# A decode kernel bound by its K/V stream: MLP weights moved ahead of the stream, wo and w4 behind it, and PE's tile work written as a loop

## The chip, the cores and the metric

The kernel runs on one core of one Trainium2 chip. The metric is device time in microseconds (us). A kernel was run several times, and the kernel before was always run beside it on the same chip. Repeated runs of one kernel agree within 0.5% (most within 0.3%). Engines are named as the profile names them: PE (matrix products), PEld (its weight loads), DVE (vector), ACT (scalar), POOL and SP (here the engine that issues the transfers). "DMA engine" means one of the 16 hardware engines that carry the transfers of this core.

## The reference, cut to what matters

One token is decoded. There are two branches on the same normalised input, and both are added to it.

```python
xn = _layernorm(x)
# A: grouped-query attention over a cache: 32 query heads, 4 K/V heads, 65536 positions, width 128
q = xn @ wq                                   # 1024 x 4096
o = softmax(q k^T / sqrt(128)) v              # K and V: 67 MB each
A = o @ wo                                    # 4096 x 1024
# B: mixer MLP with one position, so the shifted h is all zeros
hs = shift(gelu(layernorm(xn) @ w1)) @ w2     # 1024 x 1024 each
x1 = xn + hs
B = x1 + gelu(layernorm(x1) @ w3) @ w4        # 1024 x 3584 and 3584 x 1024
return x + A + B
```

All data is bf16. 169.87 MB must be read and only 2 KB written.

## The kernel before

The cache is cut into 32 tiles (`NT`) of 8192 positions, and two tiles make one K transfer and one V transfer of 4 MB. DVE transposes each half of K into `X` (`Ttr`), PE forms the scores (`QK`), DVE and ACT do the running softmax, PE and DVE transpose the probabilities (`PTr`), PE multiplies them by V (`PV`), and POOL accumulates (`FLASH`). Each buffer `Kn` and `Vn` has two slots. The MLP and output weights travel between the K/V transfers into a buffer `W` of their own, and their products stand between the tiles:

```python
w_seq = [(0, w1_dma, 3, w1_pe), (4, w2_dma, 7, w2_pe),
         (8, lambda: w3_dma(0), 11, lambda: w3_pe(0)), (12, lambda: w3_dma(1), 15, lambda: w3_pe(1)),
         (16, lambda: wo_dma(0), 19, lambda: wo_pe(0)), (20, lambda: wo_dma(1), 23, lambda: wo_pe(1))]
...
for n in range(NT):
    h, nb = divmod(n, NSUB)
    QK(n); Ttr(n + 1, [0]); stats1(n)
    if nb == 0 and h > 0: combine_1(h - 1)          # the finished head, while the next one runs
    MB(n); stats2(n); EXP(n); Ttr(n + 1, [1])
    if nb == 0 and h > 0: combine_2(h - 1)
    PTr(n); Ttr(n + 1, [2, 3]); PV(n); FLASH(n)
    ...                                             # products and transfers of w_seq, next K or V
wo_pe(2); combine_1(3); combine_2(3); wo_pe(3)
for i in range(4): w4_pe(i)
```

The last pair of tiles is loaded in two halves each of K and V (`if m < NPAIR - 1: ... else: for hf in range(2)`).

## Time and profile before

| what | kernel before |
|---|---|
| time, median of 3 runs | 402.89 us (402.85 to 402.98) |
| profiled span | 401.7 us |
| data read | 169.87 MB |
| DMA engines busy, 13 to 385 us | 100% |
| last w4 part fully landed | 398.8 us |
| last product on PE ends | 399.4 us |

The page of the profile for the kernel before, parts 1 to 4 in extract. Part 1 gives the busy us of each engine (share of the span), part 2 the mean busy share of the DMA engines in 40 slices (9 is 90% or more), part 3 packets, MB and share of the 16 DMA engines' time by queue, part 4 the chain that ended last.

```profile
span 401.7 us, 4776 instructions
PE 186.4 (46%) x1859; PEld 78.5 (20%) x1875; DVE 228.4 (57%) x401; ACT 48.9 (12%) x128; POOL 61.8 (15%) x90
DMA  8999999999999999999999999999999999999994
...
q1 hardware_dynamic: 6920, 169.87, 98.4%
q8 instruction: 15, 0.25, 0.2%
q14 instruction: 8, 0.07, 0.0%
...
DMA 55%; DVE 24%; PE 16%; issue 2%; ACT 1%; SPq 0%; another core or an unknown queue 0%; POOL 0%; ACTq 0%
```

No compute engine is above 57%, and the DMA row has no hole between its first and last slice: the transfers set the time. The two ends can change it. The view by windows shows the far end. The columns are the window, its length, the busy us of PE, PEld, DVE, ACT and POOL with instruction counts, the granted share of PE's clock, the DMA share and GB/s.

```profile
390.00:393.00 3.00, 2.63 (x52) 1.74 (x56) 0.00 (x0) 0.00 (x0) 0.00 (x0) 0.50 0.97 412
393.00:396.00 3.00, 1.15 (x44) 0.69 (x36) 0.00 (x0) 0.00 (x0) 0.00 (x0) 0.99 0.88 371
396.00:399.00 3.00, 1.43 (x32) 0.48 (x24) 0.00 (x0) 0.00 (x0) 0.00 (x0) 0.58 0.32 128
399.00:402.00 3.00, 0.44 (x8) 0.00 (x0) 0.42 (x1) 0.00 (x0) 0.00 (x0) 0.50 0.00 1
```

The DMA share does not drop from 1 to 0 at once; it falls to 0.88 and 0.32 over 5 us. Some of the 16 DMA engines have finished their part while others have not, and a transfer is of use only when all have: the last product below starts at 398.85 us, 0.04 us after the last landing. The trace records 16 landings for each transfer, one for each DMA engine. These are the landings of one transfer near the start, one in the middle and the last w4 part, in us after the first of the 16:

```
lands at 32.2   0  0.05 0.11 0.12 0.16 0.17 0.20 0.23 0.25 0.26 0.27 0.29 0.30 0.32 0.33 0.38
lands at 234.6  0  0.11 0.24 0.29 0.33 0.66 0.85 1.53 1.57 1.61 1.61 1.63 1.64 1.67 1.68 1.87
lands at 398.8  0  0.10 0.15 0.21 0.43 0.71 1.12 1.31 1.58 2.79 2.86 2.89 2.90 2.94 2.98 3.44
```

The spread grows in steps, and each large step follows an instruction packet: the packet on queue q8 (16 KB of PE's program) holds one DMA engine for about 0.9 us, and the next 32 KB packet of that engine then takes, in most cases, about 1.7 us instead of 1.21.

The timeline of the tail (start, length, engine, line, operation, tiles, shapes, count, and in brackets the idle time before it and what ended it) shows the products of the last combine (which merges the partial sums of one K/V head), then PE waiting for each part of w4, then a copy; the store follows:

```profile
384.67 1.16 PE L564 MATMUL M_ps<-O_acc,cb_W 128*128 128x128 f32 x8 [0.78 <-DVE cb_W L557]
386.92 1.88 PE L404 MATMUL OUT_ps<-W,o_bf 128*1 128x256 bf16 x32 [1.09 <-DVE o_bf L571]
390.37 2.98 PE L404 MATMUL OUT_ps<-Kn,gh_bf 128*1 128x256 bf16 x56 [1.58 <-DMA Kn<-in_B_w_dram]
395.21 1.04 PE L404 MATMUL OUT_ps<-Kn,gh_bf 128*1 128x256 bf16 x32 [1.85 <-DMA Kn<-in_B_w_dram]
397.63 1.02 PE L404 MATMUL OUT_ps<-Kn,gh_bf 128*1 128x256 bf16 x16 [1.38 <-DMA Kn<-in_B_w_dram]
398.85 0.59 PE L404 MATMUL OUT_ps<-Kn,gh_bf 128*1 128x256 bf16 x8 [0.19 <-DMA Kn<-in_B_w_dram]
399.50 0.42 DVE L631 CAST orow<-OUT_ps 128x256 bf16<-128x256 f32 x1 [12.73 <-PE OUT_ps L404]
```

### The profile page before, as it was taken

To read this page: it belongs to the slowest core of one execution; us is meant where nothing else is said; L and a number is where in the kernel's file an instruction comes from. 1 tells how busy PE (TensorE), PEld (TensorE's weight loads), DVE (VectorE), ACT (ScalarE), POOL (GpSimd) and SP (SyncE) were. 2 spreads that over 40 slices of the span, in tenths; PEclk is the share of its full clock that TensorE was granted. 3 is DMA by queue.
4 is the path that set the end of the run, shared out by engine and by line. 5 is a ranking of instruction groups with operands and counts; after the bars stand their busy time and mean duration, and the time that the engine had idled before them with its cause. 6 is when DMAs were issued, how large, how long until landed. Compare 5 with 4: busy or idle time off the path is not lost.

```text
span 401.7 us, 4776 instructions
## 1 busy us (share of the span) xinstructions
PE 186.4 (46%) x1859; PEld 78.5 (20%) x1875; DVE 228.4 (57%) x401; ACT 48.9 (12%) x128; POOL 61.8 (15%) x90
## 2 busy tenths in 40 slices
PE   0332325064525745285531965353433654444664
PEld 0211101021103511062110731121111311111132
DVE  0247566277816578255744287576836775788410
ACT  1000111011101011011110011111201111112100
POOL 5000003012211011110310101111110112112110
PEclk9985556556565556555655555656555656565566
DMA  8999999999999999999999999999999999999994
GB/s 359 424 418 438 445 418 424 460 419 421 436 447 419 429 435 435 422 436 445 420 428 450 426 419 441 441 419 428 434 439 421 447 432 424 426 425 436 437 416 207
DMA packets 7087, 170.19 MB, mean 424 GB/s; under 512 B 916, under 2 KB 920, under 8 KB 1048
## 3 DMA queue, kind: packets, MB, share of 16 engines
q1 hardware_dynamic: 6920, 169.87, 98.4%
q8 instruction: 15, 0.25, 0.2%
q14 instruction: 8, 0.07, 0.0%
q10 hardware_dynamic: 144, 0.00, 0.0%
HBM read 169.87 MB, written 0.00 MB: 423 GB/s over the span
## 4 chain that ended last, share of the span: by engine, by line
DMA 55%; DVE 24%; PE 16%; issue 2%; ACT 1%; SPq 0%; another core or an unknown queue 0%; POOL 0%; ACTq 0%
DMA Kn<-in_A_k_cache_dram 44%; DVE X L476 13%; DMA Kn<-in_B_w_dram 6%; DMA Vn<-in_A_wq_dram 5%; PE H_ps L366 4%; PE S_ps L488 3%; DVE pT_f L529 3%; PE OT_ps L536 3%; DVE mrow L495 3%; PE M_ps L366 1%; ACT p_sb L518 1%; PE PT_ps L527 1%; PE M_ps L564 1%; PE OUT_ps L404 1%; DVE Yall L393 1%
## 5 line engine op out<-in xcount | busy, mean ns | idle before, releaser
L476 DVE STREAM_TRANSPOSE X<-Kn 128x1024 f32<-128x1024 f32 x128 | 151.7, 1215 | 67.4 <-DMA Kn<-in_A_k_cache_dram 67.4
L536 PE MATMUL OT_ps<-Vn,pT_f 128*32 128x512 bf16 x512 | 60.7, 627 | 52.4 <-DVE pT_f L529 52.4
L488 PE MATMUL S_ps<-X,Yall 128*32 128x512 bf16 x512 | 59.1, 608 | 16.1 <-DVE X L476 16.1
L501 PE MATMUL MB_ps<-Rm,Lmat 128*128 128x16 bf16 x32 | 6.1, 192 | 90.1 <-DVE Rm L496 90.1
L550 POOL TENSOR_TENSOR O_acc<-O_acc,tmpO 128x513 f32<-128x513 f32 x28 | 32.8, 1172 | 88.6 <-ACT tmpO L544 88.6
L518 ACT ACTIVATE p_sb<-S_ps,brun 128x512 bf16<-128x512 f32 x32 | 22.0, 687 | 192.7 <-DVE brun L516 157.3
L548 POOL TENSOR_SCALAR O_acc<-O_acc,ff 128x513 f32<-128x513 f32 x28 | 19.5, 698 | 153.4 <-ACT ff L523 153.4
L495 DVE TENSOR_REDUCE mrow<-S_ps 128x1 f32<-128x512 f32 x32 | 21.6, 674 | 25.5 <-PE S_ps L488 25.5
L544 ACT ACTIVATE tmpO<-OT_ps 128x512 f32<-128x512 f32 x32 | 19.1, 598 | 108.0 <-PE OT_ps L536 108.0
L488 PEld LDWEIGHTS S_ps<-X,Yall 128*32 128x32 bf16 x512 | 16.6, 126 | 54.7 <-DVE X L476 38.2
L529 DVE STREAM_TRANSPOSE pT_f<-PT_ps 128x512 f32<-128x512 f32 x32 | 22.9, 716 | 6.1 <-PE PT_ps L527 4.2
L536 PEld LDWEIGHTS OT_ps<-Vn,pT_f 128*32 128x32 bf16 x512 | 14.6, 129 | 59.2 <-DVE pT_f L529 42.0
L501 PEld LDWEIGHTS MB_ps<-Rm,Lmat 128*128 128x128 bf16 x32 | 3.3, 102 | 114.9 <-DVE Rm L496 114.9
L527 PE MATMUL PT_ps<-p_sb,permR 128*128 128x512 bf16 x16 | 9.3, 580 | 21.4 <-ACT p_sb L518 21.4
L366 PEld LDWEIGHTS H_ps<-xn_bf,W 128*128 128x128 bf16 x224 | 14.4, 169 | 1.7 <-issue 1.7
L366 PE MATMUL H_ps<-xn_bf,W 128*128 128x1 bf16 x224 | 14.5, 202 | 0.0
L527 PEld LDWEIGHTS PT_ps<-p_sb,permR 128*128 128x128 bf16 x32 | 3.4, 105 | 41.4 <-ACT p_sb L518 41.4
L505 DVE TENSOR_REDUCE Bst<-MB_ps 128x1 f32<-128x16 f32 x32 | 5.6, 174 | 8.3 <-PE MB_ps L501 8.3
L330 PE MATMUL M_ps<-ln_s,ones_f 128*128 128x1 f32 x6 | 1.8, 362 | 17.3 <-DVE ln_s L329 17.3
L546 POOL COPY O_acc<-tmpO 128x513 f32<-128x513 f32 x4 | 2.4, 612 | 47.4 <-ACT tmpO L544 47.4
L404 PE MATMUL OUT_ps<-Kn,gh_bf 128*1 128x256 bf16 x112 | 5.6, 364 | 5.0 <-DMA Kn<-in_B_w_dram 5.0
L631 DVE CAST orow<-OUT_ps 128x256 bf16<-128x256 f32 x1 | 0.4, 425 | 12.7 <-PE OUT_ps L404 12.7
(109 smaller groups left out, 116.6 us busy)
## 6 DMA issues: line engine op xcount, KB each, us to landing
Kn<-in_A_k_cache_dram SPq DMA_DIRECT2D x15, 4096.0 KB, 27.3
Vn<-in_A_v_cache_dram SPq DMA_DIRECT2D x15, 4096.0 KB, 23.3
W<-in_B_w_dram SPq DMA_DIRECT2D x2, 3584.0 KB, 24.9
W<-in_A_wo_dram SPq DMA_DIRECT2D x3, 2048.0 KB, 23.8
Kn<-in_A_wq_dram SPq DMA_DIRECT2D x1, 4096.0 KB, 12.1
Vn<-in_A_wq_dram SPq DMA_DIRECT2D x1, 4096.0 KB, 21.2
W<-in_B_w_dram SPq DMA_DIRECT2D x2, 2048.0 KB, 33.8
Kn<-in_A_k_cache_dram SPq DMA_DIRECT2D x2, 2048.0 KB, 25.3
```

The costliest lines, as they stand in the source:

```text
L366: fns.append(lambda e, j=j, cx=cx: e.matmul(ps_tile[:, c0 + cx:c0 + cx + 1], lhs_fn(j - j0, cx), rhs_fn(j), start=(j == 0 and cx == 0), st ...
L404: fns.append(lambda e, lhs=lhs, rhs=rhs, jj=jj: e.matmul(OUT_ps[32 * jj:32 * jj + 1, 0:256], lhs, rhs[:, 256 * jj:256 * jj + 256], start=F ...
L476: _op(q_dve, lambda e, ix=ix: e.transpose(out=X32[:, xs, 1024 * ix:1024 * (ix + 1)], in_=Kn32[:, s, 4096 * half + 1024 * ix:4096 * half + ...
L488: fns.append(lambda e, we=we, cm=cm, mv=mv: e.matmul(S_ps[32 * cm:32 * cm + 32, :], Yall[:, h, we, :, :].rearrange("p a g -> p (a g)"), mv ...
L495: _op(q_dve, lambda e: e.reduce_max(mrow[:, m:m + 1], S_ps[:, :], axis=AX.X), reads=[b_S], writes=[b_mrow[m]])
L518: _op(q_act, lambda e: e.activation(p_sb[:, m, :], S_ps[:, :], ACTF.Exp, bias=brun[:, kn:kn + 1], scale=SCALE, accum_out=tmpO[:, m, 512:513]),
L527: _op(q_pe, lambda e: e.matmul(PT_ps[:, :], permR[:, :], p_sb[:, m, :], start=True, stop=True), reads=[b_p[m], b_const], writes=[b_PT])
L529: _op(q_dve, lambda e: e.transpose(out=pT_f[:, :], in_=PT_ps[:, :]), reads=[b_PT], writes=[b_pT])
L536: fns.append(lambda e, q=q, q4=q4: e.matmul(OT_ps[32 * q4:32 * q4 + 32, :], pT_bf[:, q, :, 1], Vn[:, s, 8192 * half + 512 * q:8192 * half ...
L544: _op(q_act, lambda e: e.activation(tmpO[:, m, 0:512], OT_ps[:, :], ACTF.Copy), reads=[b_OT], writes=[b_tmpO[m]], partial=True)
L548: _op(q_pool, lambda e: e.tensor_scalar(out=O_acc[:, :], in0=O_acc[:, :], scalar1=ff[:, m:m + 1], scalar2=0.0, op0=ALU.mult, op1=ALU.add), ...
L550: _op(q_pool, lambda e: e.tensor_tensor(out=O_acc[:, :], in0=O_acc[:, :], in1=tmpO[:, m, :], op=ALU.add), reads=[b_tmpO[m]], writes=[b_Oacc])
```

## The change

The MLP's w1, w2 and w3 are now loaded ahead of K and V into the still empty K, V and X slots; wo and w4 come after the stream; the buffer W is gone. The MLP products use the activation row as the stationary operand and the weights as the moving one (`mm_rows`), 128 products instead of 352. What is left between the tiles is the same for every four tiles, so PE runs it as a loop of eight passes, with waits on registers. All four combines and all wo products come after the loop. The residual, which PE added before, is now added by the last DVE instruction. The core of the diff, abridged (`...` and some lines drawn together):

```diff
-        W = sb("W", [P, 14336], BF)
+        Ycur = sb("Ycur", [P, 4, 4, G], BF)
+        idle = sb("idle", [P, 1], F32)
+        rrow = sb("rrow", [P, 256], F32)
+        rres = sb("rres", [P, 256], F32)
-        O_acc = sb("O_acc", [P, 513], F32)
+        O_all = sb("O_all", [P, HKV, 513], F32)
...
+        load_rows(Kn[:, 0, 0:8192], [b_K[0][0]], "w1", B_w1, 0, 8)
+        load_rows(Kn[:, 0, 8192:16384], [b_K[0][1]], "w2", B_w2, 0, 8)
+        load_rows(Xf[:, 0:4 * F], b_X[0] + b_X[1], "w3a", B_w3, 0, 4)
+        load_rows(Vn[:, 0, 0:4 * F], b_V[0], "w3b", B_w3, 4, 4)
...
-            if m < NPAIR - 1:
-                _dma(...)                                   # whole K or V
-            else:
-                for hf in range(2): _dma(...)               # the last ones in halves
+            _dma(...)                                       # always whole
...
+            if n % 4 == 0:
+                q_pe.mark()
             QK(n)
...
-            if nb == 0 and h > 0: combine_1(h - 1) / combine_2(h - 1)
-            if n in at_pe: at_pe[n]()
-            if n in at_dma: at_dma[n]()
...
-        wo_pe(HKV - 2); combine_1(HKV - 1); combine_2(HKV - 1); wo_pe(HKV - 1)
+        q_pe.mark()
+        for h in range(HKV):
+            combine_1(h)
+            combine_2(h)
+        for h in range(HKV):
+            wo_pe(h)
...
-        q_pe.emit(nc.tensor)
+        q_pe.emit_rolled(nc.tensor, es)
```

PE's program shrinks from 3894 to 1345 instructions.

## The prediction

> What bounds the kernel. The per-window table of engine busy time shows the DMA engines 100-101% busy at 430-436 GB/s in every window from 13 to 385 us; the page counts 169.87 MB, the queue share of the data is 98.4%, and no other engine is above 57% (DVE). The waits of DVE for K transfers (67 us) and the chain of waits (DMA 55%) say the same: compute keeps up, the transfers set the time. Outside the full-rate stretch lie about 2 us of start and 3 us after the last landing (product 0.6, copy 0.42, store). Data at 432 GB/s takes 393 us, so at most about 5 us can be gained.
>
> Where those us are. Every transfer lands on the 16 DMA engines separately. In the trace the 16 landings of one transfer lie within 0.4 us until 43 us; from then the last lags the first by 1.9 us (54 us), 3.2 (256 us), 3.4 us (the last w4 part). The jumps follow the instruction queue of PE: 15 packets of 16 KB, one per 256 or so PE instructions, each pushing one DMA engine about 1.5 us back, eight engines in turn, most of them twice. The busy share falls to 0.88 and 0.32 in 393-396 and 396-399 us: DMA engines waiting for the slowest. The kernel therefore loses about 3 us to PE's instruction stream.
>
> What the change does.
> - Bytes of data: none saved. w1-w3 go first, wo and w4 last; the queue should stay full: six transfers (19.9 MB, 46 us) are issued at once, K0 follows at about 22 us, K1 near 40, V1 near 55.
> - PE's program shrinks from 3894 to 1345 instructions (352 one-column products become 128, eight tile rounds become one). Read once, that is 5 fetches rather than 15: last lag about 1.5-2 us, end about 1.6 us earlier.
> - The loop body has 308 PE instructions, more than one 256-instruction block. The Trainium skill, "Runtime: NRT & Kernel Launch", section Instruction fetch mechanics, says that a taken branch whose target is outside the current two-page window fetches the page before going on; it also gives PE more IRAM than the others. The trace of before cannot tell whether the loop stays resident. If not: 2-3 fetches per pass, 20-26 in all, the last lag 4.5-6 us, end 1-3 us later; if they always hit the same DMA engines, 8 hits of 1.5 us, end up to 9 us later. The stall at the branch itself hides in the 7 us of slack per pass (38.8 us of transfers against 31 of work).
> - The tail: four combines (about 2.7 us each by the durations before), 128 wo and 112 w4 products now follow the last tile. K15 lands about 351 us, PV of the last tile ends near 374, combines 385, wo 392, w4 within 1 us of the last landing. No loss expected if PE's clock rises in that run, up to 1.5 us otherwise.
>
> Critical path: only the DMA end and the 3 us after it. Prediction: loop resident (about 55%) 401.2 us, otherwise 404-407, rarely 411. I say 401.8 us, range 399.6 to 406.5; faster by over 2% 0.02, within 2% 0.92, slower by over 2% 0.06.
>
> What shows it: 16-engine landing spread at the end (about 2 us if right, over 4 if the loop refetches); instruction packets in the DMA queue table (5-6 against 15, or over 20); DMA share 1.0 in all windows up to 390 us; last product within 1 us of the last landing.
>
> What would make it wrong: a dry queue while the w3 products hold buffers, the loop refetching, or the lengthened PE tail ending after the transfers.

## More of the kernel before

SBUF tensors are laid out in the order in which they are declared; nothing asks for an alignment:

```python
...                                  # some sixty small tensors
W = sb("W", [P, 14336], BF)
X = sb("X", [P, 2, 8192], BF)
Kn = sb("Kn", [P, 2, 16384], BF)
Vn = sb("Vn", [P, 2, 16384], BF)
```

## The result and the profile after

The changed kernel takes 406.63 us (median of 4 runs, 406.37 to 407.37), the kernel before 402.87 us. The ratio is 1.0095, with a 95% interval of 1.0081 to 1.0109. A ratio here is the mean time of one kernel's runs over that of the other's of the same rounds, so it is not quite the ratio of the medians. The change is a small, clear loss, within 2%.

The page of the changed kernel, the same parts (PE's instruction packets are those on q8):

```profile
span 405.2 us, 4445 instructions
PE 185.2 (46%) x1587; PEld 61.5 (15%) x1587; DVE 235.4 (58%) x423; ACT 51.1 (13%) x136; POOL 62.1 (15%) x90
DMA  8999999999999999999999999999999999999992
...
q1 hardware_dynamic: 6632, 169.87, 97.9%
q8 instruction: 5, 0.08, 0.1%
q14 instruction: 8, 0.07, 0.0%
...
DMA 56%; DVE 22%; PE 15%; ACT 4%; issue 2%; SPq 0%; POOL 0%; ACTq 0%
```

Two forecasts hold here. PE's instruction packets fell from 15 to 5, so the loop does not fetch its body again on each pass. And the DMA row has no hole, so no transfer queue ran dry. Still the span is 3.5 us longer. The landings in the two traces split it:

| in the profiled run, us | before | changed | difference |
|---|---|---|---|
| first DMA engine finishes the last w4 part | 395.36 | 397.32 | +1.95 |
| spread from the first to the last DMA engine | 3.44 | 3.95 | +0.51 |
| from the last landing to the end of the span | 2.85 | 3.90 | +1.04 |
| span | 401.66 | 405.16 | +3.50 |

First row: even the DMA engine that nothing held up is 2 us later, with the same bytes and no hole. It was slower throughout. 4 MB transfers land every 9.72 us in the changed kernel and about every 9.67 us before. Packets of 32 KB took 1213 ns in 4035 of 4096 cases before; in the changed kernel most took 1216 or 1224 ns (mean 1220 against 1217, with the few long ones).

Second row: PE's fetches are down to five, yet the last DMA engine lags more. The landings of the last w4 part are now

```
lands at 401.3  0  0.08 0.10 0.11 0.13 0.21 0.23 0.24 0.26 0.65 0.78 1.41 1.45 1.70 1.88 3.95
```

Fifteen DMA engines are within 1.9 us, better than before, and one is alone at the back. Its lag grew by about 0.95 us at each of three times (153, 262 and 361 us from the start), and at each time there is a packet of 8 KB on queue q14, where the programs of the other engines are read.

Third row: windows and timeline of the tail, columns as before.

```profile
393.00:396.00 3.00, 2.83 (x64) 1.53 (x59) 0.85 (x3) 0.00 (x0) 0.00 (x0) 0.72 0.96 399
396.00:399.00 3.00, 2.52 (x80) 1.80 (x84) 0.00 (x0) 0.00 (x0) 0.00 (x0) 1.00 0.53 210
399.00:402.00 3.00, 2.67 (x96) 1.87 (x84) 0.00 (x0) 0.00 (x0) 0.00 (x0) 1.00 0.03 14
```

```profile
375.17 1.90 PE L609 MATMUL OT_ps<-Vn,pT_f 128*32 128x512 bf16 x16 [0.88 <-DVE idle L545]
377.00 0.59 PE L627 MATMUL M_ps<-O_all,Dmat_f 128*128 128x1 f32 x2
379.23 2.07 PE L637 MATMUL M_ps<-O_all,cb_W 128*128 128x128 f32 x8 [1.64 <-DVE cb_W L630]
383.11 2.08 PE L637 MATMUL M_ps<-O_all,cb_W 128*128 128x128 f32 x8 [0.78 <-DVE cb_W L630]
387.01 2.08 PE L637 MATMUL M_ps<-O_all,cb_W 128*128 128x128 f32 x8 [0.78 <-DVE cb_W L630]
390.90 2.08 PE L637 MATMUL M_ps<-O_all,cb_W 128*128 128x128 f32 x8 [0.78 <-DVE cb_W L630]
392.91 1.88 PE L493 MATMUL OUT_ps<-Kn,o_bf 128*1 128x256 bf16 x32
...
398.57 1.70 PE L493 MATMUL OUT_ps<-Kn,gh_bf 128*1 128x256 bf16 x56 [0.16 <-PE OUT_ps L493]
400.44 1.04 PE L493 MATMUL OUT_ps<-X,gh_bf 128*1 128x256 bf16 x32 [0.16 <-PE OUT_ps L493]
401.64 0.61 PE L493 MATMUL OUT_ps<-X,gh_bf 128*1 128x256 bf16 x16 [0.16 <-PE OUT_ps L493]
402.42 0.39 PE L493 MATMUL OUT_ps<-X,gh_bf 128*1 128x256 bf16 x8 [0.17 <-PE OUT_ps L493]
402.86 0.58 DVE L692 TENSOR_TENSOR orow<-OUT_ps,rres 128x256 bf16<-128x256 f32 x1 [8.93 <-PE OUT_ps L493]
```

None of the w4 products waits for a transfer any more; before, all four groups did. From 399 us nearly all DMA engines are idle (share 0.03) while PE is still working. The combines stand one after the other, 3.9 us from one to the next, each time with PE waiting for DVE's `cb_W`, and PE ends 1.54 us after the last landing, where it ended 0.63 us after it before. The last DVE instruction, which now adds the residual too, takes 0.58 us instead of 0.42. These two, 0.91 and 0.16 us, are the third row.

### The profile page after: what moved, and what is told of

It reads as the page before. It is cut to its first block, busy times and chain, and to the rows that moved or that the text cites. A ratio compares the mean times of both kernels' runs of the same rounds, so it can differ in the third digit from the quotient of the medians. Undisturbed runs are those within 1.5% of the kernel's fastest.

```text
span 405.2 us, 4445 instructions
## 1 busy us (share of the span) xinstructions
PE 185.2 (46%) x1587; PEld 61.5 (15%) x1587; DVE 235.4 (58%) x423; ACT 51.1 (13%) x136; POOL 62.1 (15%) x90
## 3 DMA queue, kind: packets, MB, share of 16 engines
q1 hardware_dynamic: 6632, 169.87, 97.9%
HBM read 169.87 MB, written 0.00 MB: 419 GB/s over the span
## 4 chain that ended last, share of the span: by engine, by line
DMA 56%; DVE 22%; PE 15%; ACT 4%; issue 2%; SPq 0%; POOL 0%; ACTq 0%
DMA Kn<-in_A_k_cache_dram 50%; DVE X L550 11%; DMA Vn<-in_A_wq_dram 5%; PE S_ps L561 4%; ACT p_sb L591 3%; DVE pT_f L602 3%; DVE mrow L568 3%; PE PT_ps L600 2%; PE OUT_ps L493 2%; PE M_ps L637 2%; PE MB_ps L439 1%; PE MB_ps L574 1%; DVE Yall L481 1%; DVE Bst L578 1%; DVE Rm L569 1%
## 5 line engine op out<-in xcount | busy, mean ns | idle before, releaser
L550 DVE STREAM_TRANSPOSE X<-Kn 128x1024 f32<-128x1024 f32 x128 | 151.9, 1216 | 64.6 <-DMA Kn<-in_A_k_cache_dram 64.6
L561 PE MATMUL S_ps<-X,Ycur 128*32 128x512 bf16 x512 | 59.6, 613 | 20.8 <-DVE X L550 20.5
L623 POOL TENSOR_TENSOR O_all<-O_all,tmpO 128x513 f32<-128x513 f32 x28 | 33.2, 1187 | 93.9 <-ACT tmpO L617 93.9
L621 POOL TENSOR_SCALAR O_all<-O_all,ff 128x513 f32<-128x513 f32 x28 | 19.5, 697 | 133.9 <-ACT ff L596 133.9
L600 PE MATMUL PT_ps<-p_sb,permR 128*128 128x512 bf16 x32 | 18.1, 564 | 44.9 <-ACT ff L596 44.9
L561 PEld LDWEIGHTS S_ps<-X,Ycur 128*32 128x32 bf16 x512 | 14.8, 125 | 66.5 <-PE OT_ps L609 37.4
L619 POOL COPY O_all<-tmpO 128x513 f32<-128x513 f32 x4 | 2.4, 611 | 51.7 <-ACT tmpO L617 51.7
L637 PE MATMUL M_ps<-O_all,cb_W 128*128 128x128 f32 x32 | 8.3, 441 | 4.0 <-DVE cb_W L630 4.0
L455 DVE STREAM_TRANSPOSE O_all<-tmpO 128x256 f32<-128x256 f32 (+1 forms) x3 | 2.0, 668 | 13.9 <-ACT tmpO L452 13.9
L637 PEld LDWEIGHTS M_ps<-O_all,cb_W 128*128 128x128 f32 x32 | 7.1, 328 | 4.3 <-DVE cb_W L630 4.3
L412 POOL TENSOR_TENSOR ln_s<-ln_s,neghalf 128x1 f32<-128x1 f32 x3 | 1.7, 558 | 36.3 <-DVE ln_s L410 36.3
```

The lines of the kernel that those rows point to most:

```text
L550: _op(q_dve, lambda e, ix=ix: e.transpose(out=X32[:, xs, 1024 * ix:1024 * (ix + 1)], in_=Kn32[:, s, 4096 * half + 1024 * ix:4096 * half + ...
L561: fns.append(lambda e, we=we, cm=cm, mv=mv: e.matmul(S_ps[32 * cm:32 * cm + 32, :], Ycur[:, we, :, :].rearrange("p a g -> p (a g)"), mv, s ...
L600: _op(q_pe, lambda e: e.matmul(PT_ps[:, :], permR[:, :], p_sb[:, m, :], start=True, stop=True), reads=[b_p[m], b_const], writes=[b_PT])
L621: _op(q_pool, lambda e: e.tensor_scalar(out=O_all[:, h, :], in0=O_all[:, h, :], scalar1=ff[:, m:m + 1], scalar2=0.0, op0=ALU.mult, op1=ALU ...
L623: _op(q_pool, lambda e: e.tensor_tensor(out=O_all[:, h, :], in0=O_all[:, h, :], in1=tmpO[:, m, :], op=ALU.add), reads=[b_tmpO[m]], writes= ...
L637: fns.append(lambda e, t=t: e.matmul(M0_ps[:, 128:256], cb_W[:, t, :, :].rearrange("p g i -> p (g i)"), O_all[:, h, t * P:(t + 1) * P], st ...
```

## The experiments

From the table come three theories. Layout: the big buffers lie at another address, and each packet is a little slower. `Kn` starts at byte 98048 of a partition before, a multiple of 256; in the changed kernel at 77856, which is 32 more than one. `X` and `Vn` moved likewise (`W` is gone). Straggler: the last DMA engine is the one that takes DVE's instruction fetches, whatever PE does. Tail: what follows the landing of the last K transfer has become a chain that the last landing no longer hides. The rivals are that the new order of the stream or the loop itself makes transfers slower, that PE's fetches still set the end, and that waits on registers slow the tile chain. All results were correct; each kernel ran beside the kernel before on one chip.

### Where the buffers start

Three kernels differ from the changed one, or from the one before, only in an unused tensor ahead of the big ones:

```diff
+        pad_sb = sb("pad_sb", [P, 8], F32)      # after_pad32, before X;  before_off32, before W
+        pad_sb = sb("pad_sb", [P, 56], F32)     # after_pad224, before X
```

> The changed kernel with 32 bytes per partition of unused SBUF ahead of the big buffers X, Kn and Vn, so that they start at 64 modulo 256 bytes instead of 32 (in the kernel before: 0). Layout theory (the removed and added small tiles moved the big buffers off their boundary, and every 32 KB packet takes 1216-1224 ns instead of 1213): if 64 bytes is the boundary that counts, packets go back to 1213 ns, a 4 MB transfer lands every 9.67 us instead of 9.72, the end comes about 2 us earlier, near 404.6 us. If 256 bytes is the boundary, as the Trainium skill's account of reads suggests, nothing changes: 406.6. Rival (the new order of the stream, or the loop, slows the transfers): nothing changes, 406.6.

> The changed kernel with 224 unused bytes ahead of the big buffers, so that they start at 0 modulo 256 as in the kernel before. Layout theory in both forms: packets of 1213 ns, 9.67 us per 4 MB, about 2 us less, near 404.6 us; still slower than before because the last DMA engine lags by 4 us and the PE tail ends about 1 us after the last landing. Rival (order of the stream or loop): 406.6 us.

> The kernel before with 32 unused bytes ahead of W, X, Kn and Vn, so that they start at 32 modulo 256. Layout theory: packets of 1216-1224 ns, 9.72 us per 4 MB, about 2 us slower: near 404.9 us. Rival: 402.9 us, unchanged, since order and unrolled PE program are those of before.

| kernel | start modulo 256 | most frequent times of a 32 KB packet | last w4 part: first and last landing | time | ratio to before |
|---|---|---|---|---|---|
| before | 0 | 1213 ns | 395.36, 398.81 us | 403.03 us | 1 |
| changed (measured earlier, before then 402.87) | 32 | 1216, 1224 | 397.32, 401.27 | 406.63 | 1.0095 |
| after_pad32 | 64 | 1215, 1222 | 396.70, 400.79 | 406.80 | 1.0094 |
| after_pad224 | 0 | 1213 | 395.33, 398.74 | 405.11 | 1.0048 |
| before_off32 | 32 | 1216, 1224 | 397.22, 401.18 | 405.30 | 1.0058 |

The layout theory holds in both directions. 32 unused bytes make the kernel before 2.3 us slower, and 224 unused bytes give the changed kernel the landings of the kernel before to within 0.1 us. Together, the order of the stream and the loop cost the transfers nothing. The spread moves with the address too: 3.42 us in after_pad224 against 3.95, and 3.96 us in before_off32 against 3.44. So the +0.51 us of the second row is alignment as well, and at the same alignment the last DMA engine lags as much after the change as before it. A start at 0 recovers the 2.5 us of the last landing, a start at 64 only 0.5 us of them and none of the time; starts at 128 were not tried. The times of after_pad224 and before_off32 came out 0.4 to 0.5 us above what was expected (404.6 and 404.9).

The Trainium skill, "DMA: Bandwidth & Descriptors", section How a descriptor splits into AXI transactions, says that a read that does not start on a 256-byte boundary begins at the boundary below and pays for the unused bytes; this is the account of reads that the first expectation means. The page says it of reads; here the written address in SBUF was moved and the read address was not, and the runs show a loss too. A 4 MB transfer, eight packets of 32 KB on each DMA engine, takes 0.05 us longer, so about 6 ns a packet; all the data are 324 such packets on each DMA engine, about 2 us (an estimate from these figures). Whether the page's cause is at work in these writes is not shown.

After alignment 2 us of loss are left, although the transfers end as early as before. The last product of after_pad224 ends 2.9 us after the last landing (398.74 us) and waits for no transfer:

```profile
401.26 0.39 PE L494 MATMUL OUT_ps<-X,gh_bf 128*1 128x256 bf16 x8 [0.16 <-PE OUT_ps L494]
```

That is the tail.

### The loop

```diff
-        q_pe.emit_rolled(nc.tensor, es)
+        q_pe.emit(nc.tensor)
```

> The changed kernel with PE's program written out instead of looped (constants in its waits). My forecast's step (PE's instruction fetches set the end) expects 13 instruction packets instead of 5 and the last landing about 1.5 us later, near 408 us. Straggler theory (the last DMA engine is the one that takes all four instruction fetches of DVE, about 0.95 us each, and PE's fetches go to others): the last lag stays near 4 us, and the time stays within 0.7 us of 406.6. Loop-overhead rival (register arithmetic and waits on registers cost the tile chain): up to 1 us faster, with tile periods of 7.6 us instead of 7.9.

The result is 406.79 us (ratio 1.0099), the same as with the loop. The queue table of after_unrolled:

```profile
q8 instruction: 12, 0.20, 0.2%
q14 instruction: 8, 0.07, 0.0%
```

Twelve instead of five fetches of PE's program moved several DMA engines back (three besides the last now lag by 3.1 us or more, where the next to last had 1.9), but the last one lags 3.98 us, as with the loop (3.95). So in the changed kernel PE's fetches did not set the end, and my forecast that fewer of them would bring it forward failed there. The loop is not harmful either. In the trace, QK starts 0.13 us after its last input ends (0.12 in the last tile) in all 31 tiles that follow another, the seven after a jump back included; with constants it is 0.10 us (0.09). Register arithmetic thus costs 0.03 us at that place, and no jump stalls.

### The tail

Both kernels start from after_pad224. One loads the last K in halves, as the kernel before did. The other overlaps the four combines.

```diff
 # pad_khalf
+            if ch == "k" and m == NPAIR - 1:
+                for hf in range(2):
+                    _dma(q_sp, chan("kh%d" % hf), ... t[:, s, 8192 * hf:8192 * hf + 8192] ..., writes=[b_t[s][hf]])
 # pad_comb: cb_W and cb_rL per head, a PSUM bank per head
-        for h in range(HKV):
-            combine_1(h)
-            combine_2(h)
+        combine_1(0, 3)              # sums of heads 0 to 2 in one product, then their cb_W
+        combine_2a(0)                # PE's part
+        combine_1(3, 1)
+        for h in range(1, HKV): combine_2a(h)
+        for h in range(HKV): combine_2b(h)      # DVE's part
```

> The aligned changed kernel (after_pad224, 405.1 us), with the last K transfer (K15) issued as two halves, as the kernel before had it. Tail theory (what is left after alignment is the chain from the landing of K15 through the last two tiles, four combines and 240 products, which ends 2.9 us after the last landing): the chain starts about 3.9 us earlier, the last product ends near the last landing (398.7 us plus 0.5), the time falls to 402.7-403.4 us. Rival (the last landing already sets the end and the copy or the store got slower): no change, 405.1.

> The aligned changed kernel, K15 whole, with the four combines overlapped instead of one after another: one product for the sums of heads 0-2, separate weights and PSUM banks per head, so that PE goes from one head's products to the next without waiting for DVE. Tail theory: the combines take about 9 us instead of 16, PE's last product again waits for the last w4 part, 402.7-403.4 us. Rival (the landing sets the end): 405.1.

A pad_comb that kept all four heads in one PSUM bank would have read a PSUM bank while PE wrote to it; the one that ran uses four banks.

The times are 402.98 us (ratio 1.0005, interval 0.9992 to 1.0019) and 403.05 us (1.0004, 0.9990 to 1.0017), against 405.11 us for after_pad224. Either cure is enough. The timeline of pad_khalf, the last three groups of w4 products only:

```profile
396.43 1.04 PE L499 MATMUL OUT_ps<-X,gh_bf 128*1 128x256 bf16 x32 [0.15 <-PE OUT_ps L499]
397.85 0.61 PE L499 MATMUL OUT_ps<-X,gh_bf 128*1 128x256 bf16 x16 [0.38 <-DMA X<-in_B_w_dram]
399.09 0.39 PE L499 MATMUL OUT_ps<-X,gh_bf 128*1 128x256 bf16 x8 [0.63 <-DMA X<-in_B_w_dram]
```

And of pad_comb, from the combines on:

```profile
377.38 2.08 PE L641 MATMUL M_ps<-O_all,cb_W 128*128 128x128 f32 x8 [1.64 <-DVE cb_W L634]
379.25 0.43 PE L630 MATMUL H_ps<-O_all,Dmat_f 128*128 128x1 f32 x2
379.54 1.96 PE L641 MATMUL S_ps<-O_all,cb_W 128*128 128x128 f32 x8
381.33 1.06 PE L641 MATMUL MB_ps<-O_all,cb_W 128*128 128x128 f32 x8
382.23 1.06 PE L641 MATMUL M_ps<-O_all,cb_W 128*128 128x128 f32 x8
...
398.85 0.60 PE L494 MATMUL OUT_ps<-X,gh_bf 128*1 128x256 bf16 x8 [0.21 <-DMA X<-in_B_w_dram]
```

In both, the last products wait for the transfer again, and the time is that of the kernel before. In pad_comb the combines' products take 5.9 us (377.38 to 383.29) where they took 13.7 (379.23 to 392.98). Part of that is PE's clock: kept busy, it does the later groups in 1.06 us instead of 2.08; the trace has the granted clock at 0.5 until 381.3 us and at 1.0 from there, 3.9 us after the first group began. In the changed kernel, with its waits, it stays at 0.5 from 374.2 to 394.7 us. The Trainium skill, "TensorE: Matmul & The Clock Gate", section What's actually happening, says that PE runs at half clock until it has been busy for about 3.4 us; the factor of two in these lines agrees, and the 3.9 us are near it.

### The straggler, and a version with all cures

Two kernels change the length of DVE's program. pad_dveplus is after_pad224 with 128 tiny instructions more. pad_best has the alignment, both cures of the tail, and 83 instructions fewer.

```diff
 # pad_dveplus
+        for i in range(128):
+            q_dve.op(lambda e, i=i: e.memset(spare[:, i:i + 1], 0.0))
 # pad_best, besides pad_khalf and pad_comb
-            _op(q_dve, ... tensor_tensor(out=dd[:, m:m + 1], in0=brun[:, kn:kn + 1], in1=brun[:, kp:kp + 1], op=ALU.subtract) ...)
-            _op(q_act, ... activation(ff[:, m:m + 1], dd[:, m:m + 1], ACTF.Exp) ...)
+            _op(q_act, ... activation(ff[:, m:m + 1], brun[:, kp:kp + 1], ACTF.Exp, bias=brun[:, kn:kn + 1], scale=-1.0) ...)
-            for we in range(4): ...                # Yall: 16 products
+            ...                                    # Yall: 4 products, one per head
```

> The aligned changed kernel with 128 more tiny DVE instructions (one-column memsets while DVE waits for the first K), one 8 KB fetch block more. Straggler theory (DVE's instruction fetches all land on one DMA engine and push it about 0.9 us each): the lag of the last DMA engine at the end rises from 3.4 to about 4.3 us, the last landing and the time by about 0.9 us, near 406 us. Rival (which engine is last is chance, or comes from PE's fetches): lag stays at 3.4 us, 405.1 us.

> Aligned, K15 in halves, overlapped combines, and 83 DVE instructions fewer (the rescale difference is formed inside the exponential on ACT, the sixteen query-mask products are four), so that DVE crosses one fetch block less before the end. Theories of layout, tail and straggler together: three DVE fetches, lag at the end about 2.5 us instead of 3.4, last landing near 397.8 us, time near 402.0 us, just faster than the kernel before (403.0). If the straggler theory is wrong: 402.7-403.4.

| kernel | DVE instructions | q14 packets | spread at the end | last landing | time |
|---|---|---|---|---|---|
| after_pad224 | 505 | 8 | 3.42 us | 398.74 us | 405.11 us |
| pad_dveplus | 633 | 9 | 4.58 | 399.81 | 406.09 |
| pad_khalf (for comparison with pad_best) | 505 | 8 | 3.58 | 399.05 | 402.98 |
| pad_best | 422 | 7 | 2.60 | 397.98 | 402.44 |

The queue tables of pad_dveplus, then of pad_best:

```profile
q8 instruction: 5, 0.08, 0.1%
q14 instruction: 9, 0.07, 0.0%
```

```profile
q8 instruction: 5, 0.08, 0.1%
q14 instruction: 7, 0.06, 0.0%
```

One DVE fetch more made the spread 1.2 us longer, and one fewer made it 1.0 us shorter than pad_khalf's, each time by way of the one DMA engine at the back (the next one lags 1.7 us in both). pad_comb, with the overlapped combines and all of DVE's fetches, has 3.57 us, so the combines do not shorten it.

The kept traces can be read further. A DMA engine's packets follow each other almost without a gap, so each packet can be joined to the one that starts where it ends. Joined so, the DMA engine that ends last carries four fetches of q14 in after_unrolled (36.2, 153.1, 262.2 and 360.4 us), five in pad_dveplus (38.2, 52.1, 153.5, 262.1 and 359.7 us, the second of them new) and three in pad_best (44.6, 182.8 and 299.8 us). By the same joining, which can mix up two DMA engines that run in step, PE's first eight fetches in the kernel before lie on eight different ones. The straggler theory holds, with about 1 us per 8 KB fetch. In pad_dveplus PE still ends 2.75 us after the last landing: the time grows because every large transfer, K15 too (352.79 against 351.75 us), lands with the slowest DMA engine.

pad_best is faster than the kernel before by a hair: 0.9987 (interval 0.9973 to 1.0000), with the landing and the spread near what was expected and the time 0.4 us above it. It was run once more, together with its unrolled form:

```diff
-        q_pe.emit_rolled(nc.tensor, es)          # pad_best_again keeps it
+        q_pe.emit(nc.tensor)                     # pad_best_unrolled
```

> pad_best with PE's program written out: about 12 PE instruction packets instead of 5, everything else the same. Here the DVE engine lags by only 2.6 us, so PE's fetches, two on some DMA engines at about 1.5 us each, can come to the front: last lag about 3.1 us, time about 0.5 us above pad_best, 402.9 us. If PE's fetches do not matter at all: 402.4, as pad_best.

> pad_best once more, on the same chip as pad_best_unrolled, for the comparison: 402.3-402.6 us, last lag about 2.6 us. If it comes out at or above the kernel before, its gain was chance.

pad_best_again: 402.30 us, ratio 0.9982 (0.9968 to 0.9996), spread 2.44 us in the kept trace. pad_best_unrolled: 402.75 us, ratio 0.9995 (0.9981 to 1.0008), 13 PE packets, spread 3.27 us with five DMA engines between 2.50 and 3.27 us. Here, with DVE's engine further forward, PE's fetches do come to the front. The difference of the medians is 0.45 us, and that of the last landings in the kept traces 0.66 us (397.91 against 398.57). The two intervals overlap, but of five runs each the fastest unrolled one (402.52 us) is level with the slowest looped one (402.53). So the loop is worth about half a microsecond in this kernel.

## Why the prediction was wrong

The forecast was 401.8 us with a range up to 406.5; measured were 406.63 us. It saw the size of the possible gain rightly (a few us at the ends) and said "within 2%", but it put the time on the wrong side of the kernel before, and the range missed it.

The step that failed is "Read once, that is 5 fetches rather than 15: last lag about 1.5-2 us, end about 1.6 us earlier". The five fetches came, the earlier end did not: at equal alignment the lag is 3.42 us against 3.44 before, because the last DMA engine is held by DVE's fetches. Two costs were missing or too small: the address of the buffers (2.5 us in the last landing) and the tail (1.04 us after it, where none was expected or "up to 1.5 us"). From the forecast's 401.2 us for a resident loop, 1.6, 2.5 and 1.0 us lead to 406.3; the profiled run took 406.40. In detail:

- "What bounds the kernel": right. The DMA share stays at 1 in all long windows of both kernels, and everything that changed the time did so through the last landing or what follows it.
- "Bytes of data: none saved ... the queue should stay full": right, but the step stopped there. It took the rate of 432 GB/s as given. The term that was missing is the address of the buffers: about 2 us in the first DMA engine's landing (1.95), 2.5 us in the last landing (401.27 against 398.74), shown by padding in both directions. The addresses could have been read from the built programs before any run.
- "The kernel therefore loses about 3 us to PE's instruction stream" and "Read once, that is 5 fetches rather than 15: last lag about 1.5-2 us": the count was right (5 packets), the lag was not (3.95 us, and 3.42 when aligned). The step treated the lag as a matter of how many fetches there are. It is set by the DMA engine that is held longest, and in the changed kernel that is the one with DVE's. The queue q14 with its 8 packets stood in the table and I did not ask where they land. When PE was unrolled again the time stayed the same.
- "The loop body has 308 PE instructions": the doubt was whether it stays resident. It does; five packets in all, and no stall at the seven jumps. The half of the forecast's range that was kept for the other case did not arise, and the measured 406.63 lies close to it only by chance.
- "The tail ... combines (about 2.7 us each ...)": mis-sized. They measured 3.9 us each, because all their products ran at half clock (2.08 us a group; in the kernel before two of the four took 2.08 and two 1.16, the last one among them) and PE waits for DVE between them. "up to 1.5 us otherwise" was the case: PE's last product ended 1.54 us after the last landing, and the span lost 1.04 us against before. With the transfers aligned the tail alone costs 2 us (405.11 against 403.0). That K15 is no longer loaded in halves was left out of the estimate as a term; putting the halves back recovers all of the 2 us.

The sum for the changed kernel is then: alignment +2.5 (1.95 in the first DMA engine's landing and 0.5 in the spread), tail +1.04 us on the span of the profiled runs. The lag of the last DMA engine adds nothing else: at equal alignment it is as long in the kernel before, so the forecast's gain did not come. These do not simply add when cured one at a time, since landing and tail hide each other. Aligned and with either tail cure, the new order and the loop come out at 403.0 us, just where the kernel before is. What the reordering itself gains or loses is therefore not distinguishable from zero; pad_best's small gain comes with DVE's shorter program, which is no part of the change. The kernel before with a shorter DVE program was not tried. Its trace has six DMA engines between 2.79 and 2.98 us behind the first and the last at 3.44, so it could gain some 0.5 us at most that way (an estimate from these landings).

What stays open: no label tells which of the eight or so packets on q14 belong to which engine's program (DVE's were told by adding and removing DVE instructions, and by joining packets); why DVE's fetches go to one DMA engine while PE's go round eight was not tried; nor is it shown why a start off the boundary lengthens the spread as well.

## What to carry to other kernels

When transfers fill the span, look at the landings of each DMA engine, not only at the mean share: the end is set by the slowest one, and a program's own instruction fetches can be what holds it back. Start large transfer buffers on a 256-byte boundary of SBUF (starts at 32 and 64 were slower here, 128 was not tried) and check it after any change to the small tensors. Work moved behind a stream is free only as long as the chain from the last big landing to the end stays shorter than the transfers that still follow; measure that chain with the durations that it will have there (clock, waits between engines), and keep the last load in pieces.

## What the Trainium skill lacked or had wrong

- "DMA: Bandwidth & Descriptors", How a descriptor splits into AXI transactions: speaks of reads only. The runs show a cost for the SBUF address that is written: 32 KB packets of 1213 ns at 0 modulo 256, mostly 1216 and 1224 ns at 32, 1215 and 1222 ns at 64; at 32 the last landing of 169.87 MB comes 2.4 to 2.5 us later.
- No page says what an instruction fetch costs the data on the same DMA engine, or how fetches are spread over the DMA engines. Here 16 KB of PE's program puts one DMA engine back by about 1.5 us, 8 KB of DVE's by about 1 us; PE's fetches go round eight DMA engines, DVE's pile up on one.
- "Runtime: NRT & Kernel Launch", Instruction fetch mechanics: calls the instruction memory a window of two pages, and says in the same place that PE has 128 KiB. The loop of 308 PE instructions, more than one 256-instruction block, ran eight passes with five fetches in the whole program and no stall at a jump (0.13 us from the last input to QK at the tiles after one). This does not decide between the two figures: a loop of 308 can lie in two blocks of 256, and where it begins in its block is not known here.
- The same section calls fetches mostly hidden. No stall of PE shows (with the program written out, QK still starts 0.10 us after its last input), but the transfers pay: 0.45 us between looped and unrolled PE in the best version.
